# Opening of a fused attention and gated-MLP kernel: order of the first row tiles' copies and products, and width of the first weight loads

## The chip, the cores and the metric

The kernel runs on one core of one Trainium2 chip. The metric is device time in microseconds (us) of one execution, of which the median over several runs is compared. Beside the runs there is one profiled execution; its trace has a span, counted from the first to the last instruction, and a device time of its own that is a little longer than the span.

## What is computed

The input x has 2048 rows of 640 numbers (bfloat16). Each row is normalised to xn. Two branches read xn, and their product is added to x:

```
xn = layernorm(x)
s  = A(xn)                  # 32 heads of 192: q = xn @ wq, softmax over the last 512 keys of the cache, @ wo
g  = silu(B(xn))            # B: (sigmoid(xn @ w_gate) * (xn @ w_up)) @ w_down, inner width F = 1536
out = x + s * g
```

The change lies in the first 16 us of the kernel, in the opening of branch B. What matters there is the layer norm of the first 512 rows, their transposition, and the first products with `w_gate` and `w_up`.

## The kernel before

Branch B runs first, in four stages of 512 rows; the attention branch, with 16 runs of scores, values and output products, comes behind it. Within a stage of branch B the 1536 columns of the two weights are taken in 12 blocks f of 128: five products with the gate weight and five with the up weight (the 640 inputs are five chunks c of 128) fill two PSUM banks, ScalarE (ACT) takes the sigmoid of the gate half (L454) and VectorE (DVE) multiplies it with the up half (L455). The order of the work on every engine is the order in which the code is written (`manual_schedule`); the engines wait for each other only where a tile is needed.

The first stage can't wait for all 512 rows, so its opening is written out by row tiles q = 0 to 3 of 128 rows each:

- **Loads.** All go out on the sync engine's (SP) queue, in the written order. `load_x(t)` (L276) fetches row tile t of x, 160 KB. `load_w` (L297) fetches the columns between two entries of `f_cuts` (L291) of one weight for all five chunks, in 640 runs (128 partitions, 5 chunks each). A cut of 128 columns makes runs of 256 bytes, 160 KB in all; a cut of 384 columns makes runs of 768 bytes. The order is x0, x1, gate and up of block 0, x2, gate and up of block 1, x3, gate and up of block 2, and then cuts of 384 columns. Behind them on the same queue stand the next stage's rows (L281), `w_down` (L308) and seven loads that look for the largest entry of `wq` (L175).
- **Normalisation on DVE.** `ln_part` and `ln_stats` make the statistics of a tile in two halves (L324) and combine them (L329). ACT takes the square root (`ln_sqrt`, L368, the "root" of the change), DVE inverts it (L385) and `ln_apply` writes xn (L339). The order on DVE puts the first half of the statistics of tile q+1 ahead of the inversion for tile q. So the inversion and the application for tile 1 stand behind an instruction that reads x2.
- **Turning.** `turn(q)` is five transposes of 128 x 128 on TensorE (PE, L375) into one of two PSUM banks, and ACT copies from there to xnT (L377): one copy of all five chunks, or for q = 0 one of two chunks and one of three.
- **Products.** `first_mm(q, f)` is the ten products (L362) of row tile q with block f of both weights, 128 rows wide, for the first FA = 3 blocks, so twelve groups of ten in all. From block 3 on the products are 512 rows wide (L449).
- **Filling.** `warm_up(n)` puts n products of a zero tile, 512 wide, on PE (L352): nine at the very start and two behind `turn(0)`.

On ACT the order is: root 0, root 1, copies of tile 0, root 2, copy 1, root 3, copy 2, copy 3. On PE it is: nine fillers, turn 0, two fillers, and then, writing "1.0" for row tile 1 with block 0: 0.0, turn 1, 0.1, 1.0, turn 2, 1.1, 0.2, 1.2, 2.0, turn 3, 2.1, 2.2, 3.0, 3.1, 3.2.

Of the kernel before, what the change touches and what calls it, by code (L numbers as in the profile page):

```python
# [17 lines left out]
def kernel(  # L18
# [14 lines left out]
    P = 128  # L33
# [22 lines left out]
    G = 2  # L56
    NG = NPAIR // G
    assert NG >= 3
    NWARM = (9, 2)
    FA = 3  # L60
    PC = 3
    GC = 2 * G * DH
# [187 lines left out]
    with ExitStack() as bctx:  # L250
# [23 lines left out]
        def load_x(t):  # L274
            x_sb = xin_pool.tile([P, D], BF16, name=f"x_sb{t}")
            nc.sync.dma_start(x_sb[:], xf[t * P:(t + 1) * P, :])  # L276
            x_tiles[t] = x_sb[:]
# [10 lines left out]
        wu_sb = wB.tile([P, NCD, F], BF16, name="wu_sb")  # L288
        wg_r = B_w_gate.rearrange("(c p) f -> p c f", p=P)
        wu_r = B_w_up.rearrange("(c p) f -> p c f", p=P)  # L290
        f_cuts = [0, P, 2 * P, 3 * P, 6 * P]  # L291
        while f_cuts[-1] < F:
            f_cuts.append(min(F, f_cuts[-1] + 3 * P))

        def load_w(w_sb, w_r, k):
            f = slice(f_cuts[k], f_cuts[k + 1])
            nc.sync.dma_start(w_sb[:, :, f], w_r[:, :, f])  # L297
# [3 lines left out]
        for k in range(len(f_cuts) - 1):  # L301
            load_w(wg_sb, wg_r, k)
            load_w(wu_sb, wu_r, k)
            if k < 2:
                load_x(2 + k)
        wd_sb = wB.tile([P, NF, D], BF16, name="wd_sb")
        load_x4(1)
        nc.sync.dma_start(wd_sb[:], B_w_down.rearrange("(f p) d -> p f d", p=P))  # L308
# [12 lines left out]
        def ln_part(t, i):  # L321
            if i == 0:
                stats_t[t] = bwork.tile([P, nsub, nc.vector.BN_STATS_DIM], F32, name="stats")
            nc.vector.bn_stats(stats_t[t][:, i, :], x_tiles[t][:, i * fsz:(i + 1) * fsz])  # L324

        def ln_stats(t, i0=0):
            for i in range(i0, nsub):
                ln_part(t, i)
            nc.vector.bn_aggr(mv[:, t, :], stats_t[t][:])  # L329
# [5 lines left out]
        def ln_apply(t):  # L335
            xn = xpool.tile([P, D], BF16, name="xn")
            cuts = [0, 2 * P, D] if t == 0 else [0, D]
            for d in map(slice, cuts, cuts[1:]):
                nc.vector.tensor_scalar(  # L339
                    xn[:, d], x_tiles[t][:, d], mv[:, t, 0:1], rstd[:, t, :],  # L340
                    op0=ALU.subtract, op1=ALU.mult,
                )
            return xn
# [6 lines left out]
        def warm_up(n):  # L350
            for _ in range(n):
                nc.tensor.matmul(w_ps, lhsT=warm[:, 0:P], rhs=warm[:], start=True, stop=True)  # L352

        warm_up(NWARM[0])

        gu_first = [bank2() for _ in range(FA)]

        def first_mm(q, f):
            r = slice(q * P, (q + 1) * P)
            for i, w in enumerate((wg_sb, wu_sb)):  # L360
                for c in range(NCD):
                    nc.tensor.matmul(  # L362
                        gu_first[f][:, i, r], lhsT=w[:, c, f * P:(f + 1) * P], rhs=xnT[0][:, c, r],
                        start=(c == 0), stop=(c == NCD - 1),
                    )

        def ln_sqrt(q):
            nc.scalar.activation(  # L368
                rstd[:, q:q + 1, :], mv[:, q:q + 1, 1:2], AF.Sqrt, bias=eps_t[:], scale=1.0
            )  # L370

        def turn(q):
            pT = pT_banks[:, q % 2, 0:NCD * P // 2].bitcast(BF16).rearrange("p (c n) -> p c n", c=NCD)
            for c in range(NCD):
                nc.tensor.transpose(pT[:, c, :], xn_t[q][:, c * P:(c + 1) * P], ident[:])  # L375
            for cs in ((slice(0, 2), slice(2, NCD)) if q == 0 else (slice(0, NCD),)):
                nc.scalar.activation(xnT[0][:, cs, q * P:(q + 1) * P], pT[:, cs, :], AF.Copy)  # L377
# [4 lines left out]
        for q in range(TQ):  # L382
            if q + 1 < TQ:
                ln_part(q + 1, 0)
            nc.vector.reciprocal(rstd[:, q:q + 1, :], rstd[:, q:q + 1, :])  # L385
            xn_t[q] = ln_apply(q)
            if q + 1 < TQ:
                ln_stats(q + 1, 1)
                ln_sqrt(q + 1)
            if q == 0:  # L390
                turn(0)
                warm_up(NWARM[1])
                continue
            first_mm(q - 1, 0)
            turn(q)
            first_mm(q - 1, 1)
            if q == 2:
                first_mm(0, 2)
                first_mm(1, 2)
            elif q == 3:  # L400
                first_mm(2, 2)
        for f in range(FA):
            first_mm(TQ - 1, f)

# [471 lines left out]
```

The softmax here doesn't subtract the row's maximum and nothing guards it: scores larger than these inputs give would overflow.

## Time and profile before

| | |
|---|---|
| device time, 4 runs | median 903.44 us (903.22 to 903.64) |
| profiled execution | 903.56 us, its span 901.8 us |
| busy in the span | PE 891.2 us, DVE 652.2, ACT 432.8, POOL (GpSimd) 179.7 |
| bytes from and to memory | 57.87 MB read, 5.24 MB written |
| one product 128 x 128 x 128 of the opening (L362), start to start within a group | 0.056 us |
| root (L368), one copy of five chunks (L377), one application to 640 columns (L339) | 0.29, 0.70, 0.45 us |
| share of the DMA engines busy from 2 to 8 us, by whole microseconds | 0.87, 0.84, 1.06, 1.03, 1.06, 1.05 |

How to read it: an engine's busy share says who works most, but the opening is a chain in which loads, DVE, PE and ACT follow each other, and is read in order of time. In a timeline each line has the start, the length, the engine, the source line, what is written and read, how many instructions are merged into the line, and in brackets how long the engine sat idle before it and what released it. The duration of a product includes its way through the array; successive ones overlap, so the distance of the starts counts. A chain of waits in order of time has start, length and the step. In a view of DMA queues a line gives the packets, the megabytes and the time that the packets took as a share of 16 engines over the window. "SPq" is SP issuing a load; the load lands later.

### The profile page before, as it was taken

What the parts mean: (1) busy time and instruction counts of PE and PEld (TensorE: products, weight loads), DVE (VectorE), ACT (ScalarE), POOL (GpSimd) and SP (SyncE); (2) the same over time, 40 slices, a digit from 0 to 9 for tenths busy, and PEclk for the clock granted to TensorE, in tenths of its full rate; (3) what the DMA queues carried; (4) which work ended last, traced back from release to release, by engine and by line L of the source; (5) the groups of instructions that cost most, each with busy time, mean ns of one, the idle gap of its engine ahead of it and who ended that gap; (6) DMA issues with size and microseconds to landing.
All of it is one profiled execution on the core that took longest, in us unless ns stands there. A gap on an engine that the chain in (4) does not pass through costs nothing.

```text
span 901.8 us, 18481 instructions
## 1 busy us (share of the span) xinstructions
PE 891.2 (99%) x7711; PEld 531.8 (59%) x7791; DVE 652.2 (72%) x1093; ACT 432.8 (48%) x511; POOL 179.7 (20%) x222
## 2 busy tenths in 40 slices
PE   9999999999999999999999999999999999999998
PEld 5545454565656565656565656566666666565665
DVE  5879956777677866786778677866786678666566
ACT  4323346754247633753375437643854285424240
POOL 0051212771001100110011001100110000001983
PEclk9999999999999999999999999999999999999999
DMA  9993374425544645374626362727192715263744
GB/s 283 267 269 95 97 147 100 123 53 89 91 86 61 142 80 97 60 143 71 107 58 145 58 118 47 156 54 124 36 167 45 132 25 127 41 119 129 163 125 121
DMA packets 188357, 100.38 MB, mean 111 GB/s; under 512 B 156208, under 2 KB 180656, under 8 KB 188272
## 3 DMA queue, kind: packets, MB, share of 16 engines
q1 hardware_dynamic: 159088, 57.77, 32.3%
q0 software_dynamic: 9408, 29.93, 14.2%
q10 hardware_dynamic: 19776, 11.49, 5.3%
q8 instruction: 61, 1.00, 0.5%
q14 instruction: 24, 0.20, 0.1%
HBM read 57.87 MB, written 5.24 MB: 70 GB/s over the span
## 4 chain that ended last, share of the span: by engine, by line
PE 97%; DVE 1%; issue 1%; DMA 0%; ACT 0%; SPq 0%; POOL 0%; DVEq 0%
PE ps_all L716 22%; PE ps_all L565 20%; PE ps_all L673 19%; PE ps_all L655 18%; PE ps_all L449 11%; PE ps_all L499 6%; PE ps_all L362 1%; DMA x_sb<-in_A_x_dram 0%; ACT E L659 0%; DVE tmp L728 0%; DVE ps_all L725 0%; DVE o_sb L726 0%; SPq L297 0%; DVE stats L324 0%; POOL o_sb L729 0%
## 5 line engine op out<-in xcount | busy, mean ns | idle before, releaser
L659 ACT ACTIVATE E<-ps_all 128x1024 bf16<-128x1024 f32 x256 | 252.7, 1022 | 302.5 <-PE ps_all L655 255.3
L716 PE MATMUL ps_all<-wo_g,oT 128*128 128x128 bf16 (+2 forms) x1479 | 225.0, 295 | 3.3
L655 PE MATMUL ps_all<-qT,kT 64*128 64x512 bf16 x1536 | 194.3, 376 | 0.0
L673 PE MATMUL ps_all<-v_sb,E 128*128 128x193 bf16 x2048 | 189.8, 247 | 0.1
L673 PEld LDWEIGHTS <-E 128*128 128x128 bf16 x2048 | 168.6, 98 | 18.7 <-issue 6.8
L716 PEld LDWEIGHTS <-oT 128*128 128x128 bf16 x1542 | 122.0, 98 | 77.7 <-issue 2.1
L603 DVE TENSOR_TENSOR qT<-ps_all,qp 128x512 bf16<-128x512 f32 x165 | 109.7, 688 | 46.0 <-PE ps_all L565 39.4
L586 DVE COPY qp<-ps_all 128x512 f32<-128x512 f32 x150 | 100.7, 688 | 58.3 <-PE ps_all L565 58.3
L655 PEld LDWEIGHTS <-kT 64*128 64x128 bf16 x1536 | 75.3, 94 | 89.4 <-issue 5.2
L680 DVE TENSOR_TENSOR o_st<-ps_all,rden 128x768 bf16<-128x768 f32 x120 | 114.9, 957 | 5.0 <-DMA oT<-o_st 0.9
L202 POOL DMA_DIRECT2D raw<-in_A_wq_dram x80 | 47.9, 604 | 275.7 <-ACT wB L224 238.3
L135 POOL DMA_DIRECT2D k_sb<-in_A_k_cache_dram x32 | 32.7, 1026 | 271.2 <-DVE o_st L680 151.3
L219 ACT ACTIVATE raw<-raw,w_sc 128x1536 f16<-128x1536 bf16 x37 | 58.3, 1575 | 2.0 <-DMA raw<-in_A_wq_dram 1.2
L499 PE MATMUL ps_all<-wd_sb,hT_sb 128*128 128x128 bf16 (+1 forms) x377 | 52.4, 298 | 0.4
L565 PE MATMUL ps_all<-XB,wB 64*128 64x512 f16 x420 | 52.0, 376 | 0.0
L565 PE MATMUL ps_all<-X,w 64*128 64x512 bf16 x420 | 51.9, 376 | 0.0
L565 PE MATMUL ps_all<-XA,wA 64*128 64x512 f16 x420 | 51.9, 376 | 0.0
L747 DVE TENSOR_TENSOR acc_lo<-ps_all,acc_lo 128x640 f32<-128x640 f32 x48 | 39.5, 822 | 15.6 <-PE ps_all L716 15.6
L455 DVE TENSOR_TENSOR hT_sb<-ps_all,sig_sb 128x512 bf16<-128x512 f32 x48 | 32.4, 682 | 22.5 <-ACT sig_sb L454 11.8
L679 DVE RECIPROCAL rden<-ps_all 128x4 f32<-128x4 f32 x128 | 23.1, 181 | 33.6 <-PE ps_all L673 32.3
L454 ACT ACTIVATE sig_sb<-ps_all 128x512 bf16<-128x512 f32 x48 | 28.0, 596 | 40.1 <-PE ps_all L449 37.1
L747 DVE TENSOR_TENSOR acc_hi<-ps_all,acc_hi 128x640 f32<-128x640 f32 x48 | 39.3, 819 | 7.7 <-PE ps_all L716 7.7
(118 smaller groups left out, 763.6 us busy)
## 6 DMA issues: line engine op xcount, KB each, us to landing
raw<-in_A_wq_dram POOLq DMA_DIRECT2D x80, 192.0 KB, 4.0
k_sb<-in_A_k_cache_dram POOLq DMA_DIRECT2D x32, 192.0 KB, 5.6
wo_g<-in_A_wo_dram ACTq DMA_DIRECT2D x6, 960.0 KB, 7.2
v_sb<-in_A_v_cache_dram ACTq DMA_DIRECT2D x28, 192.0 KB, 3.6
gB_d<-gB_sb POOLq DMA_DIRECT2D x16, 160.0 KB, 3.8
gBa_sb<-gB_d SPq DMA_DIRECT2D x16, 160.0 KB, 3.6
xa_sb<-in_A_x_dram SPq DMA_DIRECT2D x16, 160.0 KB, 3.6
out_dram<-o_sb SPq DMA_DIRECT2D x13, 160.0 KB, 1.8
```

Source lines behind the costliest of these rows:

```text
L219: nc.scalar.activation(raw.bitcast(F16), raw, AF.Copy, scale=w_up)
L449: nc.tensor.matmul(gu[:, i, :], lhsT=w[:, c, f * P:(f + 1) * P], rhs=xnT[s][:, c, :], start=(c == 0), stop=(c == NCD - 1),)
L499: nc.tensor.matmul(oB_ps[:, d0:d0 + dsz], lhsT=hT_sb[:, f, q * P:(q + 1) * P], rhs=wd_sb[:, f, d0:d0 + dsz], start=(f == 0), stop=(f == NF ...
L565: nc.tensor.matmul(ps_all[:, b, :], lhsT=w(r, c), rhs=x[r, c, :], start=(first and k == 0), stop=(k == len(cs) - 1), skip_group_check=True,)
L586: nc.vector.tensor_copy(dst, part(b))
L603: nc.vector.tensor_tensor(q_out(i, u, pp), part(b), t, ALU.add)
L655: nc.tensor.matmul(ps[:, b, :], lhsT=kT[h, c * PC + j, :], rhs=qT_t[r][i, j][h, pp, :], start=(j == 0), stop=(j == PC - 1),)
L659: nc.scalar.activation(E_t[r, i, pp][:, c, :, :], ps, AF.Exp, scale=scale_qk)
L673: nc.tensor.matmul(o_ps[:, q // 2, q % 2, 0:DH + 1], lhsT=E[:, c, h, q * P:(q + 1) * P], rhs=vt[:, c, 0:DH + 1], start=(c == 0), stop=(c = ...
L680: nc.vector.tensor_tensor(o_st[:, :, h * DH:(h + 1) * DH].rearrange("p (b i) d -> p b i d", b=2), o_ps[:, :, :, 0:DH], rden[:].to_broadcas ...
L716: nc.tensor.matmul(oA[:, d0 - base:d0 - base + dsz], lhsT=oT_t[r, i, pp][:, q * PC + j, :], rhs=wo_t[runs[r][1]][:, cc, d0:d0 + dsz], star ...
L747: nc.vector.tensor_tensor(acc[t][:], oA[:, 0:D], acc[t][:], ALU.add)
```

## The change

It has four parts.

1. The first two blocks of both weights come in one load each: 256 columns, runs of 512 bytes, 320 KB. The order becomes x0, x1, gate of blocks 0 and 1, up of blocks 0 and 1, x2, x3, gate and up of block 2, and then as before.
2. `turn(0)`, with its two ACT copies, is written ahead of the second half of tile 1's statistics and of root 1. On ACT the order becomes: root 0, copies of tile 0, root 1, root 2, copy 1, root 3, copy 2, copy 3.
3. The two fillers behind `turn(0)` are gone; the nine at the start stay.
4. The products are taken by row tile: 0.0, 0.1, turn 1, 0.2, 1.0, 1.1, turn 2, 1.2, 2.0, 2.1, turn 3, 2.2, 3.0, 3.1, 3.2.

What is computed, and the number of products and transposes beside the two fillers, stays the same.

```
-    NWARM = (9, 2)
+    NWARM = 9
...
-        f_cuts = [0, P, 2 * P, 3 * P, 6 * P]
+        f_cuts = [0, 2 * P, 3 * P, 6 * P]
...
             load_w(wg_sb, wg_r, k)
             load_w(wu_sb, wu_r, k)
-            if k < 2:
-                load_x(2 + k)
+            if k == 0:
+                load_x(2)
+                load_x(3)
...
-        warm_up(NWARM[0])
+        warm_up(NWARM)
...
             xn_t[q] = ln_apply(q)
+            if q == 0:
+                turn(0)
             if q + 1 < TQ:
                 ln_stats(q + 1, 1)
                 ln_sqrt(q + 1)
             if q == 0:
-                turn(0)
-                warm_up(NWARM[1])
                 continue
-            first_mm(q - 1, 0)
+            for f in range(FA - 1):
+                first_mm(q - 1, f)
             turn(q)
-            first_mm(q - 1, 1)
-            if q == 2:
-                first_mm(0, 2)
-                first_mm(1, 2)
-            elif q == 3:
-                first_mm(2, 2)
+            first_mm(q - 1, FA - 1)
         for f in range(FA):
             first_mm(TQ - 1, f)
```

## The prediction

> **What bounds the kernel.** I read the page first, for who bounds the whole.
>
> ```profile
> span 901.8 us, 18481 instructions
> PE 891.2 (99%) x7711; PEld 531.8 (59%) x7791; DVE 652.2 (72%) x1093; ACT 432.8 (48%) x511; POOL 179.7 (20%) x222
> PE 97%; DVE 1%; issue 1%; DMA 0%; ACT 0%; SPq 0%; POOL 0%; DVEq 0%
> ```
>
> PE is busy for 99% and makes 97% of the chain that ended last. Behind the opening it is fed without a gap, so every later step starts as much earlier or later as the opening's last product does. The question is when that product, 3.2, ends. The chain in order of time, cut to the first microseconds, shows what it hangs on (start, length, step):
>
> ```profile
> 2.70 3.42 DMA x_sb<-in_A_x_dram
> 6.12 0.03 issue
> 6.15 0.49 DVE stats L324
> ...
> 6.74 0.45 DVE xn L339
> 7.19 0.41 DVE stats L324
> ...
> 7.62 0.22 DVE mv L329
> ...
> 7.87 0.29 ACT rstd L368
> 8.16 0.60 ACT X L377
> ...
> 8.80 0.72 PE ps_all L362 x10
> ```
>
> The opening hangs on x2. Its load is issued at 2.70 and lands at 6.12; DVE's first look at it stands ahead of tile 1's inversion and application, so xn of tile 1 is done at 7.19; then root 2, which stands ahead of copy 1 on ACT, then copy 1, then product 1.0 at 8.80. That is 1.61 behind the end of the application. From 8.80 the timeline of PE has no gap:
>
> ```profile
> 5.16 0.74 PE L375 MATMUL ps_all<-ident,xn 128*128 128x128 bf16 x5
> 5.69 0.90 PE L352 MATMUL ps_all<-warm 128*128 128x512 bf16 x2
> 6.58 0.71 PE L362 MATMUL ps_all<-X,wg_sb 128*128 128x128 bf16 x5
> 8.80 0.44 PE L362 MATMUL ps_all<-X,wg_sb 128*128 128x128 bf16 x5 [0.40 <-ACT X L377]
> 11.87 0.44 PE L375 MATMUL ps_all<-ident,xn 128*128 128x128 bf16 x5
> 12.35 0.70 ACT L377 ACTIVATE X<-ps_all 128x640 bf16<-128x640 bf16 x1 [1.81 <-PE ps_all L375]
> 14.66 0.44 PE L362 MATMUL ps_all<-X,wu_sb 128*128 128x128 bf16 x5
> ```
>
> A group of five takes 0.28 from start to start, so a `first_mm` takes 0.56 and a turn 0.28. Behind 8.80 stand ten `first_mm` and two turns: 5.60 + 0.56 = 6.16, which ends at 14.96 (the last five start at 14.66; 14.94 by that line). The turn at 11.87 gives the price of a copy that ACT can take at once: copy from 12.35 to 13.05, and with the 0.05 from a copy's end to its product that 8.75 to 8.80 shows, 1.23 from the first transpose to the first product that needs it.
>
> **Part 1, the loads.** Issues are cheap: a weight load of 640 runs holds SP for 0.43 to 0.56 whether its runs have 256 or 768 bytes, so x2 is still issued at about 2.70. What counts is the work ahead of it on the 16 DMA engines, which are full. Three windows of the DMA view, in which almost only runs of 256 bytes (3.55 to 4.00), 768 bytes (12 to 13) and 1280 bytes (2.0 to 2.9) move:
>
> ```profile
> q1 hardware_dynamic: 414, 0.10, 101.5%
> ```
> ```profile
> q1 hardware_dynamic: 483, 0.36, 109.8%
> ```
> ```profile
> q1 hardware_dynamic: 218, 0.25, 89.6%
> ```
>
> Share x 16 engines x window / packets: 17.7, 36.4 and 59 ns a packet. A run of 512 bytes isn't in the trace. Its bounds are the rows beside it, 17.7 and 36.4; I take 27, the middle in bytes and in time. Ahead of x2 stand two weight loads as now, but of 512-byte runs: 2 x 640 x (27 - 17.7) / 16 = 0.74 us more. x2 lands at 6.12 + 0.74 = 6.86 (bounds 6.12 and 7.62). The Trainium skill ("DMA: Bandwidth & Descriptors", Specifications) has it that transfers reach line rate from 512 bytes on and are slowed below; with its 27 GiB/s an engine, 512 bytes would take some 18 ns, an estimate from that page, and the sum would end at the lower bound. The 768-byte row, at 36.4 ns, is far from that rate.
>
> With x2, DVE moves: application of tile 1 done at 7.19 + 0.74 = 7.93, root 2, copy 1, product 1.0 at 7.93 + 1.61 = 9.54. Nothing else is late by the loads: x3, now ahead of block 2, lands sooner than its 7.81, and what lies behind on SP's queue (four loads of 0.71 us engine time become two of 1.08) some 0.7 sooner. Nothing on PE waits for those from 9 us on, so that gains nothing. GpSimd's queue isn't touched.
>
> **Part 2, the copies of tile 0.** The first copy now starts at 6.17, behind root 1 (5.97); the two chunks it needs are out of PE at about 5.6 (second transpose at 5.27, 0.31 long). Freed, the copies run from 5.61 and, once the fifth transpose is out, from 5.94 to 6.42 (the second takes 0.48 now); product 0.0 starts at 6.02 in place of 6.58. Up weights of blocks 0 and 1 land at 5.63 + 0.74 = 6.37, in time. Root 1 goes from 5.97 to about 6.32; the inversion that it feeds waits for x2 anyway. So 0.0 and 0.1 are done at 7.47. **This gain of 0.56 goes nowhere**: turn 1 needs xn of tile 1, at 7.93. PE stands for half a microsecond.
>
> **Part 3, the fillers.** They cost 0.90 of PE in a stretch where PE waits for the copies: nothing. Whether they hold up the clock is a rival below.
>
> **Part 4, the order by row tile.** Turn 1 from 8.05 to 8.33, product 0.2 to 8.89. Block 2's up weights land at 10.08 now. Four loads at 0.71 become two at 1.08, so they come some 0.7 sooner, 9.4; the ten products then end at about 9.7, against 1.0's 9.54: 0.16 later, or nothing if the load, whose neighbours land 0.57 apart, loses its own lag behind gate 2 (8.4). I take nothing and keep 0.16 for the range. From 1.0 on each turn has only one `first_mm` behind it before the next tile is needed: 0.28 + 0.56 = 0.84 of cover against 1.23. That is a **new stall of 0.39 at 2.0 and one at 3.0**; before, three `first_mm` stood there. xn of tiles 2 and 3 is ready long before (2 at about 9.6, its turn at 10.66).
>
> **The sum.** From 1.0 at 9.54: nine `first_mm` 5.04, two turns 0.56, two stalls 0.78, end at 15.92. Before, 14.96. That is **+0.96 us**. The profiled execution took 903.56, so it would be 904.52; it stands 0.12 above the median of 903.44, which becomes **904.4**. With the bounds of the 512-byte run: at 17.7 ns 1.0 is at 8.80, the end at 15.18, +0.22; at 36.4 ns +1.70. For scale, 0.2% of 903.44, about what a measurement of this kernel tells from no change, is 1.81 us.
>
> **Rivals.**
>
> *x2 isn't late* (chance 0.14). If 512-byte runs cost no more than 256-byte ones, or the engines had slack, only the stalls are left, less the product 0.2 that is already behind: +0.2, **903.65**. For it: the engines stood at 0.84 from 3 to 4 us. Against it: they are at 1.03 to 1.06 from 4 us on, where x2 moves.
>
> *The clock comes later* (chance 0.28). PE's products run at half speed until 6.12 at least (0.11 from transpose to transpose) and at 0.056 from 6.58, 5 us after the first filler, though the granted clock is recorded as 1.00 throughout. Without the two fillers PE stands idle from 5.8 to 6.02 and again before turn 1. If half speed lasts through row tile 0: 0.0 and 0.1 end at 8.39, turn 1 at 8.92, 0.2 at 9.99; 1.0 starts there, 0.45 late, +1.4, **904.8** (0.16). If it lasts through row tiles 0 and 1: 1.0, 1.1 to 12.13, turn 2 to 12.66, 1.2 to 13.73, so 2.0 is at 13.73 in place of 11.89: +2.8, **906.2** (0.12). Against it: the idle pieces are short beside the 4.5 us of filling. The Trainium skill ("TensorE: Matmul & The Clock Gate", Parts 1 and 4) says that full speed follows on one busy window of about 3.4 us and that transposes don't count as busy. By the page, five transposes without fillers behind them may spoil a window, and one window more is the first of these two cases; this trace, where the transposes are followed by fillers, can't show it.
>
> *Not slower* (chance 0.08): the 0.56 of part 2 is kept. It has its place at the first product and is kept if x2 lands no later than 6.12, which lets turn 1 follow at 7.47, and if the copies behind turns 2 and 3 are covered, which takes 0.84 in place of 1.23. The point from which it decides: 1.0 by 9.36 if neither turn stalls PE (14.96 less the 5.60 of work behind), by 8.58 if both do (0.78 less). All of it kept: **902.9**. Against it: the 1.23 is made of measured pieces, 0.48, 0.70 and 0.05, and even with turn 1 at 7.47 product 1.0 comes at 8.70.
>
> **How the numbers follow.** Forecast 0.50, x2 in time 0.14, half speed through tile 0 0.16, through two tiles 0.12, not slower 0.08. The range leaves out the last two, 0.20: from 903.2, a little under the lowest slower case, to 905.9, the upper bound of the run's price (905.1) with the tile-0 clock's 0.45 and the late load's 0.16 on it, 905.7, and the spread of 0.2 of single runs. Slower by over 0.2% (from 905.25): the two-tile case 0.12, two fifths of the tile-0 case 0.06 (dear runs with it), and 0.07 of the forecast with both upper bounds: 0.25. Faster by over 0.2% would need more than the 1.38 that there would be with 3.2 ending at 13.58 (6.02 and 7.56 of work, no gap at all); I leave 0.03 for what the trace doesn't show. The same: 0.72.
>
> **What would show it.** In the trace after: DVE's statistics of x2 released at about 6.9; product 0.0 at about 6.0; PE idle ahead of turn 1 for about 0.5 and ahead of 2.0 and 3.0 for 0.39 each, released by ACT's copy; the first 512-wide product about 0.9 later than 15.16 or its unseen first at 14.94. Wrong would be: statistics at 6.1, transposes spaced 0.11 at turn 1 or 2, a stall in 0.2 on block 2's up weights beyond 9.7, or a wait in later stages that isn't there now.

## The result and the profile after

The changed kernel takes 904.86 us (median of 42 runs, 904.21 to 905.70), the kernel before 903.57 (60 runs beside them, 903.16 to 904.50). The ratio is 1.0015, its 95% interval 1.0010 to 1.0019: **slower by 1.3 us**, below the 1.81 us of 0.2%, but clear of the scatter. The profiled execution took 904.88 us, its span is 903.1. The page shows the same bound as before:

```profile
span 903.1 us, 18475 instructions
PE 891.7 (99%) x7709; PEld 531.8 (59%) x7789; DVE 652.0 (72%) x1093; ACT 433.0 (48%) x511; POOL 180.0 (20%) x222
PE 97%; DVE 1%; issue 1%; DMA 1%; ACT 0%; SPq 0%; POOL 0%; DVEq 0%
```

The chain of waits in order of time, first microseconds (start, length, step); source lines behind the edit have moved by one to three:

```profile
2.71 4.77 DMA x_sb<-in_A_x_dram
7.48 0.02 issue
7.51 0.49 DVE stats L325
...
8.10 0.45 DVE xn L340
...
9.23 0.29 ACT rstd L369
9.52 0.60 ACT X L378
10.12 0.04 issue
10.16 1.28 PE ps_all L363 x20
11.44 0.29 PE ps_all L376 x5
11.73 0.02 issue
11.76 0.71 ACT X L378
12.47 0.04 issue
12.51 1.28 PE ps_all L363 x20
...
14.11 0.71 ACT X L378
...
14.86 1.83 PE ps_all L363 x30
```

Read it against the chain of before. There x2 landed at 6.12 and ACT's copies appeared once, ahead of product 1.0. Here x2 lands at 7.48, and the copies appear three times, ahead of 1.0, of 2.0 and of 3.0. PE waited for each ("PEld" is PE loading its weights). The timeline of the same kernel has the pieces:

```profile
5.98 0.77 ACT L378 ACTIVATE X<-ps_all 128x256 bf16<-128x256 bf16 x2 [1.46 <-PE ps_all L376]
6.42 0.75 PE L363 MATMUL ps_all<-X,wg_sb 128*128 128x128 bf16 x5 [0.47 <-ACT X L378]
8.60 0.45 PE L376 MATMUL ps_all<-ident,xn 128*128 128x128 bf16 x5 [0.48 <-DVE xn L340]
9.35 0.28 PEld L363 LDWEIGHTS <-wu_sb 128*128 128x128 bf16 x5 [0.19 <-DMA wu_sb<-in_B_w_up_dram]
11.28 0.44 PE L376 MATMUL ps_all<-ident,xn 128*128 128x128 bf16 x5
12.51 0.44 PE L363 MATMUL ps_all<-X,wg_sb 128*128 128x128 bf16 x5 [0.23 <-ACT X L378]
16.25 0.44 PE L363 MATMUL ps_all<-X,wu_sb 128*128 128x128 bf16 x5
```

The last five products start at 16.25; before, at 14.66. **The opening is 1.59 longer** in this pair of profiles, and the next 640 us are shifted by just that: the same ACT and DVE instructions start 1.59 later all along, in the median. From 11.28 to 12.51 are 1.23, the time from a turn's first transpose to the first product that needs it, of which one turn and one `first_mm` cover 0.84.

Single executions scatter by some tenths, so the opening is read from the trace in each experiment ("opening" below: how much later than in the profile of before the work behind it starts), and the times stand beside it. A second profile of each kernel shows the scatter.

> The kernel before once more, for the scatter between executions: x2 lands at 6.0 to 6.3 and product 1.0 starts at 8.7 to 9.0 if the landing is the same every time; if the landing scatters with the DMA engines, by some tenths more, and the opening with it.

> The changed kernel once more: x2 lands at 7.4 to 7.6 as in the three profiles with this order of the first loads, and 1.0 starts at 10.0 to 10.2; if the idle DMA engines from 3 to 5 us were chance, x2 lands at about 6.9 and 1.0 starts at about 9.55.

Before again: x2 lands at 6.35 in place of 6.12, opening +0.23, 903.46 us. The changed kernel again: x2 at 7.34, opening +1.46, 905.12 us. The opening isn't all that two profiles differ by. In the first pair a wait near 700 us, described at the end, adds 0.18, and the stretch from the start of the last product to the end of the span is 4.62 before and 4.16 after: 1.59 + 0.18 - 0.46 = 1.31, the difference of the spans (903.10 and 901.79). In the second pair the opening differs by 1.46 - 0.23 = 1.23, but the times by 1.66. Over all profiles of this document that last stretch takes 4.09 to 4.62, so a profile's opening and its time agree to about half a microsecond and no better.

### The profile page after: what moved, and what is told of

Same layout as the page of the kernel before. It is cut to its first block, busy times and chain, and to the rows that moved or that the text cites. A ratio compares the mean times of both kernels' runs of the same rounds, so it can differ in the third digit from the quotient of the medians.

```text
span 903.1 us, 18475 instructions
## 1 busy us (share of the span) xinstructions
PE 891.7 (99%) x7709; PEld 531.8 (59%) x7789; DVE 652.0 (72%) x1093; ACT 433.0 (48%) x511; POOL 180.0 (20%) x222
## 4 chain that ended last, share of the span: by engine, by line
PE 97%; DVE 1%; issue 1%; DMA 1%; ACT 0%; SPq 0%; POOL 0%; DVEq 0%
PE ps_all L713 22%; PE ps_all L562 20%; PE ps_all L670 19%; PE ps_all L652 18%; PE ps_all L446 11%; PE ps_all L496 6%; DMA x_sb<-in_A_x_dram 1%; PE ps_all L363 0%; ACT X L378 0%; ACT E L656 0%; DVE tmp L725 0%; DVE ps_all L722 0%; DVE o_sb L723 0%; SPq L297 0%; DVE stats L325 0%
```

## The experiments

**One part at a time, put into the kernel before.** The loads alone:

```
+        f_cuts = [0, 2 * P, 3 * P, 6 * P]
...
+            if k == 0:
+                load_x(2)
+                load_x(3)
```

> The kernel before with part 1 alone (512-byte runs, x2 and x3 behind both loads). If the late landing of x2 carries the loss: x2 lands at about 7.5 as in the changed kernel, product 1.0 starts at about 10.2 in place of 8.80, ten first_mm and two turns (6.16) follow without a stall, the opening ends at about 16.3: +1.4 us (+1.0 if x2 lands at 6.9). If the order by row tile carries it: about +0.0 to +0.2, since that order is not in this kernel. If the missing fillers carry it: 0.0, they are still here.

Measured: 904.53 against 903.60 us, ratio 1.0011 (1.0002 to 1.0020), opening +1.28. The timeline of this kernel:

```profile
7.43 0.49 DVE L325 BATCH_NORM_STATS2 stats<-x_sb 128x6 f32<-128x320 bf16 x1 [1.32 <-DMA x_sb<-in_A_x_dram]
10.09 0.44 PE L363 MATMUL ps_all<-X,wg_sb 128*128 128x128 bf16 x5 [0.55 <-ACT X L378]
15.95 0.44 PE L363 MATMUL ps_all<-X,wu_sb 128*128 128x128 bf16 x5
```

x2 is as late as in the changed kernel, 1.0 follows at 10.09, and from there to the last five products there are 5.86 without a stall, as in the kernel before (8.80 to 14.66). The late x2 is enough for most of the loss.

The order of the products alone:

```
+            for f in range(FA - 1):
+                first_mm(q - 1, f)
             turn(q)
+            first_mm(q - 1, FA - 1)
```

> The kernel before with part 4 alone (products by row tile, loads as before). By the cover theory: 2.0 and 3.0 each start 1.23 behind the first transpose of their turn in place of 0.84, and product 0.2 waits for block 2's up weights, which landed at 10.08 in the kernel before; 1.0 then starts at about 10.4, the opening ends at about 16.7: +1.8 us; +0.6 if these weights land at about 9. If only x2 matters, and it is on time here: +0.0 to +0.2.

Measured: 904.68 against 903.60 us, ratio 1.0012 (1.0003 to 1.0020), opening +1.17. Its chain of waits:

```profile
5.49 3.91 DMA wu_sb<-in_B_w_up_dram
9.40 0.05 issue
9.45 1.57 PE ps_all L362 x25
...
11.33 0.71 ACT X L377
...
12.09 1.28 PE ps_all L362 x20
```

x2 is on time, and the loss is there all the same: product 0.2 waits for block 2's up weights (9.40, between the two values expected), and each later turn stalls PE. 1.0 starts at 9.73; 6.38 behind it (5.60 and two times 0.39) is 16.11, where the first 512-wide product starts in the trace. That only the landing of x2 matters, the second of the two expectations, falls.

The copies of tile 0 ahead of root 1, without the two fillers:

```
             xn_t[q] = ln_apply(q)
+            if q == 0:
+                turn(0)
...
-                turn(0)
-                warm_up(NWARM[1])
```

> The kernel before with parts 2 and 3 alone (tile 0's copies ahead of root 1, no fillers behind turn 0). If x2 sets product 1.0: 0.0 starts at about 6.4 in place of 6.58, 1.0 stays at 8.8, 0.0 us (within 0.1). If the fillers hold the clock: transposes and products spaced 0.11 through tile 0 or longer, +0.4 to +1.9 us. If the head start counts: -0.2 to -0.5 us.

Measured: 903.85 against 903.60 us, ratio 1.0004 (0.9995 to 1.0013), which doesn't tell it from no change; opening +0.37. The chain shows where that comes from:

```profile
5.93 0.77 ACT X L377 x2
6.70 0.19 ACT rstd L368
...
6.91 0.17 DVE rstd L385
...
7.11 0.45 DVE xn L339
```

With x2 on time, root 1 behind the copies is what tile 1 waits for: its application starts at 7.11 in place of 6.74. This was not expected. The transposes at turn 1 are 0.056 apart, as before, so the missing fillers cost nothing.

The fillers put back into the changed kernel (`warm_up(2)` behind `turn(0)`):

> The changed kernel with the two fillers put back behind turn 0. If x2 sets the pace: they lie in PE's idle time ahead of turn 1; the opening ends as in the changed kernel, +1.3 us against the kernel before. If the clock was part of the loss: product 0.0's group is spaced 0.056 from its start, and 0.2 to 0.5 us come back, +0.8 to +1.1. If the fillers push the products: up to 0.2 more.

Measured: 904.77 against 903.60 us, ratio 1.0013 (1.0004 to 1.0022), opening +1.53. Its timeline, gate and up half of product 0.0:

```profile
6.64 0.74 PE L363 MATMUL ps_all<-X,wg_sb 128*128 128x128 bf16 x5
7.17 0.49 PE L363 MATMUL ps_all<-X,wu_sb 128*128 128x128 bf16 x5
```

The clock had no part in the loss. Here, with the fillers, the gate half takes 0.53 from start to start, its products 0.107 apart: half speed. The trace's record of the granted clock has full speed from 7.26 on, later than the 6.93 of the changed kernel without fillers, and the opening is the same, because turn 1 starts only at 8.55 and 8.60, with its transposes 0.056 apart. Over all profiles full speed is first recorded between 4.00 and 7.26 in the eight with the two fillers, and between 4.27 and 6.93 in the six without. (The column of the granted clock shows 1.00 also for the time ahead of that first record.) The Trainium skill ("TensorE: Matmul & The Clock Gate", Part 4) has it that transposes don't count as busy; no delay from five of them without fillers behind shows here, though nine fillers ahead of them mean that the rule itself isn't tested.

The three parts alone make 1.28 + 1.17 + 0.37 = 2.82 of opening, together 1.59. They don't add because they share the path: in the changed kernel product 0.2's wait and root 1 lie beside the wait for x2.

**What makes x2 late.** The changed kernel, blocks 0 and 1 again in 256-byte runs, all four loads ahead of x2:

```
+        f_cuts = [0, P, 2 * P, 3 * P, 6 * P]
...
+            if k == 1:
                 load_x(2)
                 load_x(3)
```

> The changed kernel with blocks 0 and 1 again as four loads of 256-byte runs, in the same place: gate 0, up 0, gate 1, up 1, x2, x3. The bytes ahead of x2 are the same. By the price per packet (four loads of 0.71 us against two of 1.08) x2 lands 0.67 later than in the changed kernel, at about 8.1, and the time is about +1.9 us against the kernel before. If the 512-byte runs leave engines idle that 256-byte runs would fill: x2 at 7.4 to 7.6, +1.2 to +1.4 as in the changed kernel. If only the place of x2 counted and runs of 256 bytes were as good per byte: no later than 7.0, +0.8.

Measured: 905.20 against 903.46 us, ratio 1.0019 (1.0010 to 1.0028), opening +1.88. Its timeline:

```profile
7.54 0.49 DVE L325 BATCH_NORM_STATS2 stats<-x_sb 128x6 f32<-128x320 bf16 x1 [1.62 <-DMA x_sb<-in_A_x_dram]
10.16 0.45 PE L363 MATMUL ps_all<-X,wu_sb 128*128 128x128 bf16 x5 [0.79 <-DMA wu_sb<-in_B_w_up_dram]
```

x2 lands at 7.51, about as late as with 512-byte runs (7.34 and 7.48). What is worse here is the load behind: block 2's up weights let their product start at 10.16 in place of 9.35. So the wider runs gained x2 next to nothing, but not because a byte costs the same in them. The trace has 16 completions of each load, as many as there are DMA engines, and the statistics begin with the last. The mean of x2's 16 is at 7.10 here, and at 6.51 to 6.66 in the four profiles with 512-byte runs and x2 behind them (the changed kernel's two, the loads alone, the fillers back): about 0.5 earlier, near the 0.67 expected by the price per packet. The last completion comes 0.41 behind the mean here and 0.69 to 0.92 behind it there, and that takes most of it back. The version with 256-byte runs has one profile only, and why the last completion lags isn't shown. In the windows view the engines are idle for part of the time in both; the last two columns are the share of the 16 DMA engines and GB/s. The changed kernel:

```profile
3.00:4.00 1.00, 1.00 (x4) 0.42 (x3) 0.90 (x3) 0.00 (x0) 0.00 (x0) 1.00 0.56 161
4.00:5.00 1.00, 1.00 (x4) 0.18 (x2) 0.96 (x4) 0.29 (x1) 0.00 (x0) 1.00 0.86 252
```

The run with 256-byte runs:

```profile
3.00:4.00 1.00, 1.00 (x4) 0.42 (x3) 0.97 (x4) 0.00 (x0) 0.00 (x0) 1.00 0.55 126
4.00:5.00 1.00, 0.89 (x4) 0.13 (x2) 0.96 (x5) 0.30 (x1) 0.00 (x0) 1.00 1.26 283
```

The DMA view of the changed kernel from 4.05 to 4.95, where nearly all packets have 512 bytes:

```profile
q1 hardware_dynamic: 448, 0.22, 84.8%
```

That is 0.848 x 16 x 0.90 / 448 = 27.3 ns a packet, what the prediction took; but in the same window the engines were busy for only 85%.

**The changed kernel without the late x2.** x2 loaded right behind x1:

```
         load_x(1)
+        load_x(2)
...
-                load_x(2)
```

> The changed kernel with x2 loaded right behind x1, ahead of the weights. If the landing of x2 is the whole loss of the first row tiles: xn of tile 1 is done at about 7.6 as with parts 2 and 3 alone (root 1 then sets it), but the up weights of blocks 0 and 1 land 0.5 later, at about 7.5, so turn 1 starts at about 8.4, 1.0 at about 9.6, and the opening ends at about 16.0: +0.8 to +1.1 us against the kernel before, 0.4 less than the changed kernel. If the weights are what the opening waits for: as the changed kernel, +1.3, or more.

Measured: 904.19 against 903.46 us, ratio 1.0010 (1.0001 to 1.0019), opening +0.78. About half of the loss is gone, and what is left is in the timeline:

```profile
9.06 0.45 PE L363 MATMUL ps_all<-X,wu_sb 128*128 128x128 bf16 x5 [0.25 <-DMA wu_sb<-in_B_w_up_dram]
11.70 0.44 PE L363 MATMUL ps_all<-X,wg_sb 128*128 128x128 bf16 x5 [0.23 <-ACT X L378]
14.05 0.44 PE L363 MATMUL ps_all<-X,wg_sb 128*128 128x128 bf16 x5 [0.23 <-ACT X L378]
```

The same with the old order of the products as well:

> The changed kernel with x2 right behind x1 and with the old order of the products: parts 1, 2 and 3 without the late x2 and without the uncovered turns. In the run with x2 first the opening ended 0.78 late, which is just the two stalls of 0.39. If they are what is left of the loss, less what the one first_mm brings that was already done there: turn 1 at about 7.7, 1.0 at about 9.2 behind root 2 and copy 1, 6.16 behind it, the opening ends at 15.3: +0.4 us, the price of root 1 behind the copies. If the order of the products were of no account: +0.7 as before.

Measured: opening +0.32, 904.16 against 903.48 us, ratio 1.0006 (0.9997 to 1.0015). In this profile the opening loses another 0.46 of its excess with the order, and the rest is about root 1's 0.37 from the run with part 2. But the profiled execution, with 903.50, is the shortest of eleven (up to 904.71), and the medians of the two versions are 904.19 and 904.16. So the times don't show that the old order gained anything here; only this one profile does.

**A version that is faster than both?** The chain of before says that x2 bounds it, so x2 was moved ahead there, as a single edit:

> The kernel before with one edit: x2 loaded right behind x1. If x2 bounds the kernel before as its chain says: the statistics of x2 start at 5.9 behind those of x1, xn of tile 1 is done at about 7.0, 1.0 starts at about 8.64 (turn 1 at 7.41 and 1.23): -0.2 us. If x2 is hidden there: 0.0, or +0.3 where the first weights, 0.5 later, hold product 0.0.

Measured: 903.49 against 903.46 us, ratio 1.0001 (0.9992 to 1.0009), opening +0.05. Product 1.0 does come at 8.63, but x3, now behind more, holds tile 2. The timeline of this kernel:

```profile
8.30 0.49 DVE L325 BATCH_NORM_STATS2 stats<-x_sb 128x6 f32<-128x320 bf16 x1 [0.72 <-DMA x_sb<-in_A_x_dram]
8.63 0.44 PE L363 MATMUL ps_all<-X,wg_sb 128*128 128x128 bf16 x5 [0.23 <-ACT X L378]
9.39 0.45 PE L376 MATMUL ps_all<-ident,xn 128*128 128x128 bf16 x5
```

Then also turn 1 between the gate and the up half of product 0.0, with copy 1 ahead of root 2:

```
+            if q == 1:
+                first_mm(0, 0, (0,))
+                turn(1)
+                first_mm(0, 0, (1,))
```

> The kernel before with x2 right behind x1, turn 1 between the gate and the up half of product 0.0, and copy 1 ahead of root 2 on ACT. By the same chain turn 1 starts at about 7.15, copy 1 at 7.6, product 1.0 at about 8.4; ten first_mm and two turns follow: the opening ends 0.4 us earlier than in the kernel before, -0.4 us. If root 2, now behind copy 1, makes tile 2 late: -0.2 to 0.0.

Measured: 903.49 against 903.46 us, ratio 1.0001 (0.9992 to 1.0010), opening -0.06; 1.0 at 8.42, but turn 2 at 9.29, again behind x3. And with x3 ahead of block 1:

> As the run before with turn 1 inside product 0.0, but with x3 loaded right behind gate and up of block 0 and so ahead of block 1. In that run 1.0 came at 8.42 and turn 2 stood until 9.29, because xn of tile 2 waited for x3 (statistics at 8.02). With x3 some 0.9 earlier (at about 7.0), turn 2 follows 1.0 at about 8.98 and the opening ends at about 14.55: -0.4 us. If block 1's weights, now later, hold product 0.1 (it ran at 7.75): -0.1 to +0.2.

Measured: 903.44 against 903.48 us, ratio 1.0000 (0.9991 to 1.0009), opening 0.00. The timeline:

```profile
8.35 0.45 PE L364 MATMUL ps_all<-X,wu_sb 128*128 128x128 bf16 x5
8.65 0.16 DVE L387 RECIPROCAL rstd<-rstd 128x1 f32<-128x1 f32 x1 [0.58 <-ACT rstd L370]
9.35 0.45 PE L377 MATMUL ps_all<-ident,xn 128*128 128x128 bf16 x5
```

Now block 1's up half runs at 8.35 in place of 8.03, and root 2, behind copy 1 on ACT, holds tile 2 until 9.35. All three expectations of a gain failed in the same way: the next row tile's x or root took the place of the wait that went. None of the three beats the kernel before.

## Why the prediction was right, and where it was not

- **PE bounds all that follows, so the opening's end decides: right**, except for a small wait near 700 us, below, and for the last stretch, which varies by half a microsecond.
- **x2 sets product 1.0: right, its size too small.** The step that failed is "2 x 640 x (27 - 17.7) / 16 = 0.74 us more". x2 came 1.36 later in the first pair of profiles. Over all profiles of the two orders of the first loads (6.12 and 6.35 before, 5.91 and 5.87 in the runs with the order of the products alone and with the early copies alone; 7.48 and 7.34 after, 7.40 and 7.42 in the runs with the loads alone and with the fillers back) it is 7.41 - 6.06 = 1.35. The price per packet was right, 27.3 ns. That the work spreads evenly over 16 full engines, on which the step rests, was not. The share of the engines from 3 to 4 and from 4 to 5 us adds up to 1.85 us in the mean of the first four profiles and to 1.59 in the other four: 0.26 less done. The mean of x2's 16 completions is at 5.55 and 6.58, 1.04 later, and the last one lags it by 0.52 and 0.83, another 0.31. An estimate from these numbers, 0.74 + 0.26 + 0.31 = 1.31, is close to the 1.35; what holds the engines and the last completion up stays open. In packets the whole would be 17.7 + 1.35 x 16 / 1280 = 34.6 ns, within the upper bound of 36.4. The range was drawn with that bound and holds the time. The rival "x2 isn't late" falls. By the rate of the Trainium skill ("DMA: Bandwidth & Descriptors", Specifications), some 18 ns for 512 bytes in the prediction's estimate from that page, x2 would have been on time; the trace doesn't agree, with its 27.3 ns.
- **From xn of tile 1 to 1.0 in 1.61: right.** The application ended at 8.55, and 1.0 started at 10.16.
- **Two new stalls of 0.39: right**, 1.23 from the first transpose to the product at both turns in each run with this order. From 1.0 on the forecast's 6.38 give 16.54; the last five products start at 16.25 and take 0.28.
- **Product 0.2's wait for the up weights: right.** 9.4 was forecast, 9.31 came (9.02 in the second profile, without a wait); the 0.16 that were left out are hidden, since 1.0 itself came at 10.16. The up weights of blocks 0 and 1, forecast for 6.37 and "in time", landed at 7.07 and held product 0.0's up half until 7.11. And x3 landed at 8.01, not sooner than 7.81. Both are hidden by the wait for x2. The 768-byte loads hold SP for 0.54 to 1.62 in the trace of before, not for 0.56 at most; x2's issue, at 2.71 as forecast, stands ahead of them.
- **Part 2 was mis-sized.** The copies were to run "from 5.61"; ACT's first copy started at 5.98, when all five transposes were out, though it reads two chunks. 0.0 started at 6.42, not at 6.02. And the edit was costed at nothing because "the inversion that it feeds waits for x2 anyway". This holds in the changed kernel, but what it costs without that cover was not given: 0.37.
- **Part 3 at nothing: right**; the rival of the clock falls with the run that puts the fillers back, in which full speed came later and the opening is the same. "Recorded as 1.00 throughout" was a misreading: in the trace of before full speed is recorded from 6.29 on.
- **Not slower: fell.** None of the head start of part 2 reached turn 1, as forecast.

In the sum: 0.96 was forecast for the opening, 1.59 and 1.46 - 0.23 = 1.23 were seen in the two pairs, 1.29 in the medians of the times. With the landing as measured the forecast's own terms give the first pair: 1.36 + 0.78 - 0.56 = 1.58 (the landing, the two stalls, and the `first_mm` 0.2 that is already done). So the excess is the landing of x2. That the times of this pair differ by 1.32, nearer to the forecast than its openings, is luck: the last stretch was 0.46 shorter.

## What to carry to other kernels

In a chain of loads, statistics, transposes and products by row tile, the first thing to count is what is issued ahead of the load that the in-order engine looks at next, and when the last piece of that load lands, not the mean; here the wider runs of the weights didn't pay for being ahead of it. The second is the cover: the time from a turn to the first product that needs it, against the work that PE has in between. Parts that each cost something alone must not be added, and a wait taken away from one tile is worth nothing if the next tile's load or root stands where it stood.

## What was not expected of the hardware

The DMA engines were busy for only 0.46 to 0.84 of the time from 3 to 4 us in the profiles of both kernels (before 0.84 and 0.53, changed 0.56 and 0.46), with weight loads issued and waiting. It isn't bound to the width of the runs, since the run with 256 bytes has 0.55, and it isn't there every time: two more runs with the loads in the order of before have 0.94 and 0.90. What keeps the engines idle there stays open.

Near 700 us DVE scales keys that have just been loaded, and waits for them. Before and with the loads alone, in the timelines:

```profile
702.71 0.62 DVE L142 TENSOR_SCALAR k_sb<-k_sb,w_sc 128x1536 bf16<-128x1536 bf16 x1 [3.13 <-DMA k_sb<-in_A_k_cache_dram]
```
```profile
704.77 0.62 DVE L142 TENSOR_SCALAR k_sb<-k_sb,w_sc 128x1536 bf16<-128x1536 bf16 x1 [3.91 <-DMA k_sb<-in_A_k_cache_dram]
```

The load that it waits for took 8.1 us from issue to landing in the one and 8.9 in the other. DVE waits 3.1 in both profiles of before, and PE is just not held up. In the changed kernel it waits 3.3 and 3.6, and the work behind it comes another 0.18 and 0.44 later; with the loads alone 3.9, 0.76 later, with PE idle for 0.6 ahead of an output product. This wait sits on an edge. DVE's wait is 2.9 to 3.2 in the seven profiles of kernels made from the one before with its cuts of the weights, and 3.3 to 3.9 in the seven with the changed kernel's cuts or with all four loads of blocks 0 and 1 ahead of x2. It doesn't go by the shift of the opening: 3.2 with the order of the products alone (1.17 late), 3.3 with x2 first and the old order (0.32 late). How the first loads could act on one 700 us later isn't shown.
